# Cross-covariance attention with a gated FFN: softmax by blocks of the output columns, q's norm folded into the copy of the scores, G/H products in another order

## The chip, the cores and the metric

One core of one Trainium2 chip. The metric is the device time of one execution in microseconds. "Batch", "chunk" (512 tokens) and "step" (one of twelve blocks of 128 hidden units, f = 0 to 11) are the loops of the kernel.

## The reference, cut to what matters

```python
# q, k, v: (4, 6016, 256) float32; tau = 1
qn = q / (norm(q, axis=1) + 1e-6)            # norms over the 6016 tokens, one per column
kn = k / (norm(k, axis=1) + 1e-6)
s  = kn.transpose(0, 2, 1) @ qn / tau        # 256 x 256 per batch
a  = softmax(s)                              # over the last axis
x  = (v @ a).reshape(24064, 256)
out = (sigmoid(x @ w_gate) * (x @ w_val)) @ w_out     # w_gate, w_val: 256 x 1536
```

## The kernel before

`v @ a @ w_gate` is made as `v @ (a @ w_gate)`: per batch, the kernel makes G = a·w_gate and H = a·w_val (twelve products of 128x512, for three column groups `fg`, two matrices and two row blocks), then runs the gated FFN on the transposed v. The scores of batch b+1 are made inside the FFN of batch b; those of batch 0 have nothing to hide behind.

```python
    psg = pool("psg", 2, space=PSUM); psv = pool("psv", 2, space=PSUM)
    pso = pool("pso", 2, space=PSUM); pss = pool("pss", 1, space=PSUM)
    psm = pool("psm", 1, space=PSUM)            # one buffer
    ...
    def sums(b):                                # row sums of exp, both column blocks, one tile
        ps_r = psm.tile([P, CB], FP32, tag="m", name="ps_r")
        for i in range(CB):
            for j in range(CB):
                mm(ps_r[:, i : i + 1], s["e"][:, j, ds(i * P, P)], ones_bf[:, 0:1], ...)
        nc.vector.tensor_scalar(out=r, in0=ps_r, scalar1=1e-9, scalar2=None, op0=ALU.add)
        nc.vector.reciprocal(r, r)
    ...
    gh_order = [(fg, w, i) for fg in range(NFG) for w in range(2) for i in range(CB)]
    ...
    copy_s(0, 0); norms_inv(0); copy_s(0, 1)    # batch 0
    busy(12); spread_k(0); busy(10)             # busy: dummy matmuls
    scale_k(0)
    transpose_v(0, 0, ...)                      # by TensorE, copied out by VectorE
    exps(0)
    nc.scalar.preload_act_table(ACT.Sigmoid)
    sums(0)
    for n in range(4): gh(0, n, ...)            # four ahead, eight in steps 0 to 7
    ...
    at(11 * FC + 0, sums, n)                    # batches 1 to 3: in chunk 11 of the batch before
    for i in range(len(gh_order)): at(11 * FC + i, gh, n, i)
```

Cuts are marked with dots; several short lines are joined.

Of the kernel before, what the change touches and what calls it, by code (L numbers as in the profile page):

```python
# [9 lines left out]
FP32 = mybir.dt.float32  # L10
# [7 lines left out]
def kernel(  # L18
# [20 lines left out]
    nc = tc.nc  # L39
# [47 lines left out]
    def mm(out, lhsT, rhs, start, stop, **kw):  # L87
        nc.tensor.matmul(out, lhsT=lhsT, rhs=rhs, start=start, stop=stop, **kw)  # L88
# [75 lines left out]
            )  # L164
        return sq

    def norm_mms(ps, sqs, nt, first, last):

        for w, sq in enumerate(sqs):
            for u in range(nt):  # L170
                for j in range(CB):
                    mm(
                        ps[:, w * CB + j : w * CB + j + 1],
                        sq[:, u, ds(j * P, P)],
                        ones_bf[:, 0:1],
                        start=(first and w == 0 and u == 0 and j == 0),
                        stop=(last and u == nt - 1),
                        skip_group_check=True,
                    )
# [54 lines left out]
            )  # L234

    def copy_s(b, j):
        s = st[b]
        if j == 0:
            s["x"] = attp.tile([P, CB, C], FP32, tag="x", name="x_sb")
        nc.vector.tensor_copy(out=s["x"][:, j, :], in_=s["s"][:, j, :])  # L240

    def scale_k(b):
        s = st[b]
        for j in range(CB):
            x = s["x"][:, j, :]
            nc.vector.tensor_tensor(out=x, in0=x, in1=s["rk"], op=ALU.mult)  # L246

    def exps(b):
        s = st[b]
        s["e"] = attp.tile([P, CB, C], BF16, tag="e", name="e_sb", bufs=2)  # L250
        for j in range(CB):
            nc.scalar.activation(
                out=s["e"][:, j, :],
                in_=s["x"][:, j, :],
                func=ACT.Exp,
                bias=shift,
                scale=s["r"][:, j : j + 1],
            )

    def sums(b):  # L260
        s = st[b]
        ps_r = psm.tile([P, CB], FP32, tag="m", name="ps_r")
        for i in range(CB):
            for j in range(CB):
                mm(
                    ps_r[:, i : i + 1],
                    s["e"][:, j, ds(i * P, P)],
                    ones_bf[:, 0:1],
                    start=(i == 0 and j == 0),
                    stop=(j == CB - 1),  # L270
                    skip_group_check=True,
                )
        r = attp.tile([P, CB], FP32, tag="rrow", name="rrow", bufs=2)
        nc.vector.tensor_scalar(out=r, in0=ps_r, scalar1=1e-9, scalar2=None, op0=ALU.add)  # L274
        nc.vector.reciprocal(r, r)
        s["rrow"] = r
        s["gh"] = [
            [ghpool.tile([P, CB, FG], BF16, tag=f"{n}{fg}", name=f"gh_{n}{fg}") for fg in range(NFG)]
            for n in ("G", "H")
        ]  # L280

    gh_order = [(fg, w, i) for fg in range(NFG) for w in range(2) for i in range(CB)]

    def gh(b, n, pl=None, tag=None, act=0):
        s = st[b]
        fg, w, i = gh_order[n]
        ps = (pl or psm).tile([P, FG], FP32, tag=tag or "m", name="ps_gh")
        for j in range(CB):
            mm(
                ps,  # L290
                s["e"][:, j, ds(i * P, P)],
                w_sb[w][fg][:, j, :],
                start=(j == 0),
                stop=(j == CB - 1),
            )
        dst = s["gh"][w][fg][:, i, :]
        r = s["rrow"][:, i : i + 1]
        if n % 2 == act:
            nc.scalar.activation(out=dst, in_=ps, func=ACT.Copy, scale=r)  # L299
        else:  # L300
            nc.vector.tensor_scalar(out=dst, in0=ps, scalar1=r, scalar2=None, op0=ALU.mult)  # L301
# [1 line left out]

    vts = {}

    def transpose_v(b, ci, ps=None):

        t0, nt = groups[ci]
        v_sb = vs.pop((b, ci))
        vT = vtpool.tile([P, TPC * CB, P], BF16, tag="vT", name="vT")  # L310
        flat = v_sb[:, :nt, :].rearrange("p t c -> p (t c)")
        if ps is None:
            nc.sync.dma_start_transpose(out=vT[:, : nt * CB, :], in_=flat)
        else:
            for n in range(nt * CB):
                nc.tensor.transpose(
                    out=ps[:, n, :], in_=flat[:, ds(n * P, P)], identity=ident_bf
                )
            nc.vector.tensor_copy(out=vT[:, : nt * CB, :], in_=ps[:, : nt * CB, :])
        vts[b, ci] = vT.rearrange("p (u cb) n -> p cb u n", cb=CB)  # L320

    hts = {}
# [52 lines left out]
    def busy(n):  # L375

        ps = psg.tile([P, CH], FP32, tag="g", name="ps_busy")
        for _ in range(n):
            mm(ps[:, :P], ones_bf, ones_bf, True, True)
# [4 lines left out]
    for g in range(last0 + 2):  # L384
        if g <= last0:
            t0, nt = groups0[g]
            sq[g] = (
                squares(0, t0, nt, 0, nc.vector),
                squares(0, t0, nt, 1, nc.vector if g == last0 else nc.scalar),
            )  # L390
            for u in range(nt):
                score(0, t0, u)
        if g >= 1:
            norm_mms(ps_n0, sq.pop(g - 1), groups0[g - 1][1], g == 1, g == last0 + 1)
    st[0]["n"] = ps_n0
    norms_sqrt(0)
    nc.scalar.preload_act_table(ACT.Exp)
    copy_s(0, 0)
    norms_inv(0)
    copy_s(0, 1)  # L400
    busy(12)
    spread_k(0)
    busy(10)
    scale_k(0)
    transpose_v(0, 0, psv.tile([P, TPC * CB, P], BF16, tag="v", name="ps_tp"))
    exps(0)
    nc.scalar.preload_act_table(ACT.Sigmoid)
    sums(0)
    for n in range(4):
        gh(0, n, *((psg, "g"), (psv, "v"))[n % 2], act=1)  # L410


    def side_work(b):

        side = {}

        def at(slot, fn, *a):
            side.setdefault(divmod(slot, FC), []).append((fn, a))

        for ci in range(NCH):  # L420
            nb, nci = (b, ci + 1) if ci + 1 < NCH else (b + 1, 0)
            lb, lci = (b, ci + 2) if ci + 2 < NCH else (b + 1, ci + 2 - NCH)
            if (nb, nci) == (0, 1):
                at(7, lambda: transpose_v(0, 1, psm.tile([P, TPC * CB, P], BF16, tag="m", name="ps_tp")))
            elif nb < B:
                at(ci * FC + 2, transpose_v, nb, nci)
            if lb < B:
                at(ci * FC + 0, load_v, lb, lci)
        n = b + 1
        if n == B:  # L430
            return side
        first, last = (14 if b == 0 else 0), 9 * FC
        for g, (t0, nt) in enumerate(groups):
            s0 = first + g * (last - first) // NCH
            at(max(0, s0 - 20), load_qk, n, t0, nt)
            for u in range(nt):
                at(first + (t0 + u) * (last - first) // NT, score, n, t0, u)
            if g == 0:
                at(s0, acc_start, n)
            for i, (fn, w) in enumerate(((acc_square, 0), (acc_add, 0), (acc_square, 1), (acc_add, 1))):  # L440
                at(s0 + 1 + 2 * i, fn, n, g, w)
        at(9 * FC + 10, norms_mm, n)
        at(9 * FC + 11, norms_sqrt, n)
        at(10 * FC + 1, norms_inv, n)
        at(10 * FC + 2, spread_k, n)
        for j in range(CB):
            at(10 * FC + 1, copy_s, n, j)
        at(10 * FC + 4, scale_k, n)
        at(10 * FC + 11, exps, n)
        at(11 * FC + 0, sums, n)  # L450
        for i in range(len(gh_order)):
            at(11 * FC + i, gh, n, i)
        return side
# [3 lines left out]
    for b in range(B):  # L457
        side = side_work(b)
        for ci in range(NCH):
            block = b + 1 < B and ci in (9, 10)  # L460
            for f in range(FC):
                glu(b, ci, f)
                flush()
                if prev is not None and not block:
                    out_mms(*prev, f * TPC, (f + 1) * TPC)
                for fn, a in side.get((ci, f), ()):
                    fn(*a)
                if (b, ci) == (0, 0) and f < len(gh_order) - 4:
                    gh(0, 4 + f, pso, "o", act=1)
            if prev is not None and block:  # L470
                for s in range(TPC):
                    out_mms(*prev, s * FC, (s + 1) * FC)
                    flush()
            prev = (b, ci)
# [38 lines left out]
```

## Time and profile before

| | before |
|---|---|
| time, median of 6 runs | 841.4 us (839.7 to 842.1) |
| span of the profiled run | 837.4 us |
| square root of batch 0's norms starts | 35.22 us |
| second chunk's first gate product starts | 55.27 us |
| first sum to first G/H product, batch 1 | 0.64 us |

Lines of the timeline read: start in us, duration in us, engine, source line, operation, output <- inputs, and in brackets the idle time of that engine just before and what ended it. PE is TensorE, PEld its weight load, DVE VectorE, ACT ScalarE. PSUM is the memory that TensorE writes its products to. The tiles: e_sb holds the exp of the scores, ps_r its row sums, rrow their inverse; ps_gh is a G or H product in PSUM, gh_G and gh_H its copies; ps_gate and ps_val are the two products of a step, g_sb the sigmoid of the first, hT the product of both; vT is the transposed v.

### The profile page before, as it was taken

The numbers are of one execution on the slowest core, as the hardware profiler recorded it, in microseconds if no ns is written. First come the engines' busy times: TensorE is split into PE (matmuls) and PEld (weight loads), VectorE is DVE, ScalarE is ACT, GpSimd is POOL, SyncE is SP. The second block draws the span as 40 slices with busy tenths as digits, with TensorE's granted clock in tenths as the row PEclk, the third lists the DMA queues.
The fourth block names the chain that finished last, engine by engine and source line by source line (L and its number), as shares of the span: only waits on it lengthen the run. The fifth ranks groups of instructions, "written<-read, shape, count | busy, mean of one in ns | idle before, by whom it ended". The sixth has DMA issues, their size and how long they took to land.

```text
span 837.4 us, 13986 instructions
## 1 busy us (share of the span) xinstructions
PE 816.6 (98%) x5327; PEld 506.3 (60%) x5338; DVE 565.3 (68%) x976; ACT 389.3 (46%) x639; POOL 83.9 (10%) x161
## 2 busy tenths in 40 slices
PE   5899999999999999999999999999999999999998
PEld 4546666665666666665566666666566565656666
DVE  2477777776667777777656777777766666666664
ACT  3554444446544444444554444444654444444442
POOL 5532100002011100000210020000000000000000
PEclk9899999999999999999999999999999999999999
DMA  9999624227655543223864353223222522322211
GB/s 176 206 206 188 131 51 89 61 51 142 119 102 107 101 108 63 48 51 89 150 136 86 88 117 78 51 76 67 58 48 51 95 51 76 76 48 68 48 35 69
DMA packets 78738, 76.65 MB, mean 92 GB/s; under 512 B 50768, under 2 KB 55632, under 8 KB 78672
## 3 DMA queue, kind: packets, MB, share of 16 engines
q0 software_dynamic: 24208, 39.33, 28.4%
q1 hardware_dynamic: 54464, 36.45, 15.8%
q8 instruction: 41, 0.67, 0.3%
q14 instruction: 25, 0.20, 0.1%
HBM read 78.64 MB, written 24.64 MB: 123 GB/s over the span
## 4 chain that ended last, share of the span: by engine, by line
PE 91%; DMA 3%; DVE 2%; ACT 1%; issue 1%; POOL 0%; ACTq 0%; POOLq 0%
PE ps_o L88 29%; PE ps_gate L88 28%; PE ps_val L88 28%; PE ps_s L88 4%; DMA k_sb<-in_k_dram 3%; PE ps_gh L88 2%; DVE hT L344 1%; ACT g_sb L343 1%; PE ps_rk L88 0%; ACT gh_H L299 0%; DVE out_sb L370 0%; PE ps_n L88 0%; DVE gh_G L301 0%; DVE gh_H L301 0%; DVE x_sb L246 0%
## 5 line engine op out<-in xcount | busy, mean ns | idle before, releaser
L344 DVE TENSOR_TENSOR hT<-ps_val,g_sb 128x512 bf16<-128x512 f32 (+1 forms) x576 | 390.9, 679 | 220.1 <-ACT g_sb L343 216.2
L343 ACT ACTIVATE g_sb<-ps_gate 128x512 bf16<-128x512 f32 (+1 forms) x576 | 338.6, 588 | 400.0 <-PE ps_gate L88 387.6
L88 PE MATMUL ps_val<-vT,gh_H 128*128 128x512 bf16 (+1 forms) x1152 | 338.1, 375 | 0.5
L88 PE MATMUL ps_gate<-vT,gh_G 128*128 128x512 bf16 (+1 forms) x1152 | 337.5, 375 | 0.5
L88 PE MATMUL ps_o<-w_out_sb,hT 128*128 128x256 bf16 x2256 | 326.1, 273 | 0.0
L88 PEld LDWEIGHTS <-hT 128*128 128x128 bf16 x2256 | 220.7, 98 | 124.8
L88 PEld LDWEIGHTS <-gh_H 128*128 128x128 bf16 x1152 | 112.7, 98 | 132.9 <-ACT gh_H L299 1.5
L88 PEld LDWEIGHTS <-gh_G 128*128 128x128 bf16 x1152 | 112.4, 98 | 37.3 <-ACT gh_G L299 0.3
L370 DVE COPY out_sb<-ps_o 128x256 f32<-128x256 f32 x188 | 78.0, 415 | 20.9 <-PE ps_o L88 20.9
L106 POOL DMA_DIRECT2D v_sb<-in_v_dram x48 | 25.5, 531 | 631.3 <-DMA vT<-v_sb 496.3
L88 PE MATMUL ps_s<-k_sb,q_sb 128*128 128x256 bf16 x376 | 72.3, 295 | 12.2 <-DMA k_sb<-in_k_dram 12.2
L88 PEld LDWEIGHTS <-q_sb 128*128 128x128 bf16 x376 | 39.1, 104 | 20.3 <-issue 7.5
L162 DVE TENSOR_TENSOR sq<-q_sb 128x1024 bf16<-128x1024 bf16 (+3 forms) x46 | 30.4, 661 | 25.3 <-PE ps_n L88 19.1
L200 DVE TENSOR_TENSOR acc<-acc,sq 128x1024 bf16<-128x1024 bf16 (+1 forms) x66 | 44.1, 669 | 0.0
L97 POOL DMA_DIRECT2D k_sb<-in_k_dram x49 | 26.9, 549 | 14.5 <-DMA k_sb<-in_k_dram 9.1
L97 POOL DMA_DIRECT2D q_sb<-in_q_dram x49 | 26.8, 548 | 13.7 <-DMA q_sb<-in_q_dram 6.3
L162 DVE TENSOR_TENSOR sq<-k_sb 128x1024 bf16<-128x1024 bf16 (+2 forms) x34 | 22.4, 658 | 0.0
L160 ACT ACTIVATE sq<-k_sb 128x1024 bf16<-128x1024 bf16 (+1 forms) x12 | 12.2, 1021 | 20.1 <-DMA k_sb<-in_k_dram 19.7
L88 PE MATMUL ps_gh<-w_gate,e_sb 128*128 128x512 bf16 x41 | 12.8, 378 | 1.6 <-DVE rrow L274 1.2
L88 PEld LDWEIGHTS <-e_sb 128*128 128x128 bf16 x112 | 9.9, 97 | 6.8 <-issue 3.2
L88 PE MATMUL ps_gh<-w_val,e_sb 128*128 128x512 bf16 x44 | 13.2, 379 | 0.4
L299 ACT ACTIVATE gh_G<-ps_gh,rrow 128x512 bf16<-128x512 f32 x12 | 8.2, 687 | 9.7 <-PE ps_gh L88 5.6
(44 smaller groups left out, 99.7 us busy)
## 6 DMA issues: line engine op xcount, KB each, us to landing
out_dram<-out_sb SPq DMA_DIRECT2D x44, 512.0 KB, 2.9
q_sb<-in_q_dram POOLq DMA_DIRECT2D x44, 256.0 KB, 6.7
k_sb<-in_k_dram POOLq DMA_DIRECT2D x44, 256.0 KB, 7.6
v_sb<-in_v_dram POOLq DMA_DIRECT2D x44, 256.0 KB, 3.9
out_dram<-out_sb SPq DMA_DIRECT2D x4, 384.0 KB, 2.4
w_gate<-in_moe_w_gate_dram POOLq DMA_DIRECT2D x3, 256.0 KB, 7.0
w_val<-in_moe_w_val_dram POOLq DMA_DIRECT2D x3, 256.0 KB, 7.6
w_out_sb<-in_moe_w_out_dram POOLq DMA_DIRECT2D x1, 768.0 KB, 13.0
```

Source lines behind the costliest of these rows:

```text
L88: nc.tensor.matmul(out, lhsT=lhsT, rhs=rhs, start=start, stop=stop, **kw)
L97: nc.gpsimd.dma_start(out=tl[:, :nt, :], in_=rows(src, b)[:, t0 : t0 + nt, :])
L106: nc.gpsimd.dma_start(out=v_sb[:, :nt, :], in_=rows(v, b)[:, t0 : t0 + nt, :])
L160: nc.scalar.activation(out=sq[:, :nt, :], in_=src[:, :nt, :], func=ACT.Square)
L162: engine.tensor_tensor(out=sq[:, :nt, :], in0=src[:, :nt, :], in1=src[:, :nt, :], op=ALU.mult)
L200: nc.vector.tensor_tensor(out=acc[:, :nt, :], in0=acc[:, :nt, :], in1=st[b]["sq", w][:, :nt, :], op=ALU.add)
L299: nc.scalar.activation(out=dst, in_=ps, func=ACT.Copy, scale=r)
L343: nc.scalar.activation(out=g_sb[:, :n], in_=ps_gate[:, :n], func=ACT.Sigmoid)
L344: nc.vector.tensor_tensor(out=hts[b, ci][:, f, :n], in0=ps_val[:, :n], in1=g_sb[:, :n], op=ALU.mult)
L370: nc.vector.tensor_copy(out=out_sb[:, s, :], in_=ps)
```

## The change

It wants the start shorter. Exp, sums and G/H products go by blocks of 128 output columns, so that block 0 can go ahead while block 1 is still in exp; q's inverse norm is multiplied in while the scores are copied out of PSUM; six G/H products instead of four stand ahead of step 0; two copies and a square are shared between VectorE and ScalarE.

```diff
-        nc.vector.tensor_copy(out=s["x"][:, j, :], in_=s["s"][:, j, :])
+        nc.vector.tensor_scalar(out=s["x"][:, j, :], in0=s["s"][:, j, :],
+            scalar1=s["r"][:, j : j + 1], scalar2=None, op0=ALU.mult)
...
-    def sums(b):
-        ps_r = psm.tile([P, CB], FP32, tag="m", name="ps_r")
+    def sums(b, i, pl=psm, tag="m"):
+        ps_r = pl.tile([P, 1], FP32, tag=tag, name="ps_r")
...
-    gh_order = [(fg, w, i) for fg in range(NFG) for w in range(2) for i in range(CB)]
+    gh_order = [(fg, w, i) for fg in range(NFG) for i in range(CB) for w in range(2)]
...  # transpose_v
-            nc.vector.tensor_copy(out=vT[:, : nt * CB, :], in_=ps[:, : nt * CB, :])
+            half = nt * CB // 2
+            nc.vector.tensor_copy(out=vT[:, :half, :], in_=ps[:, :half, :])
+            (nc.scalar.copy if late is None else late)(vT[:, half : nt * CB, :], ps[:, half : nt * CB, :])
...  # start
+    exps(0, 0); exps(0, 1)
+    nc.scalar.copy(*late.pop())
+    sums(0, 0)
+    gh(0, 0, psg, "g", act=False); gh(0, 1, psv, "v", act=True)
     nc.scalar.preload_act_table(ACT.Sigmoid)
+    sums(0, 1, pss, "s")
+    gh(0, 2, psg, "g", act=False); gh(0, 3, psv, "v", act=False)
+    gh(0, 4, pso, "o", act=True);  gh(0, 5, pso, "o", act=False)
...  # batches 1 to 3
-        at(11 * FC + 0, sums, n)
+            at(11 * FC + 0, sums, n, i)      # for i in 0, 1
```

More of the change, by code (lines that the diff above doesn't have):

```diff
@@ L165, in squares, with norm_mms @@
         return sq
-    def norm_mms(ps, sqs, nt, first, last):
-        for w, sq in enumerate(sqs):
+    def norm_mms(ps, sqs, nt, first, last, order=(0, 1)):
+        for w in order:
+            sq = sqs[w]
             for u in range(nt):
@@ L175, in norm_mms @@
                         ones_bf[:, 0:1],
-                        start=(first and w == 0 and u == 0 and j == 0),
+                        start=(first and w == order[0] and u == 0 and j == 0),
                         stop=(last and u == nt - 1),
@@ L239, in copy_s @@
             s["x"] = attp.tile([P, CB, C], FP32, tag="x", name="x_sb")
-        nc.vector.tensor_copy(out=s["x"][:, j, :], in_=s["s"][:, j, :])
-    def scale_k(b):
-        s = st[b]
-        for j in range(CB):
-            x = s["x"][:, j, :]
-            nc.vector.tensor_tensor(out=x, in0=x, in1=s["rk"], op=ALU.mult)
-    def exps(b):
-        s = st[b]
-        s["e"] = attp.tile([P, CB, C], BF16, tag="e", name="e_sb", bufs=2)
-        for j in range(CB):
-            nc.scalar.activation(
-                out=s["e"][:, j, :],
-                in_=s["x"][:, j, :],
-                func=ACT.Exp,
-                bias=shift,
-                scale=s["r"][:, j : j + 1],
-            )
@@ L260, in sums @@
-    def sums(b):
-        s = st[b]
-        ps_r = psm.tile([P, CB], FP32, tag="m", name="ps_r")
-        for i in range(CB):
-            for j in range(CB):
-                mm(
-                    ps_r[:, i : i + 1],
-                    s["e"][:, j, ds(i * P, P)],
-                    ones_bf[:, 0:1],
-                    start=(i == 0 and j == 0),
-                    stop=(j == CB - 1),
-                    skip_group_check=True,
-                )
-        r = attp.tile([P, CB], FP32, tag="rrow", name="rrow", bufs=2)
+        nc.vector.tensor_scalar(
+            out=s["x"][:, j, :],
+            in0=s["s"][:, j, :],
+            scalar1=s["r"][:, j : j + 1],
+            scalar2=None,
+            op0=ALU.mult,
+        )
@@ new lines, in scale_k, with exps @@
+    def scale_k(b, i):
+        s = st[b]
+        x = s["x"][:, :, ds(i * P, P)]
+        rk = s["rk"][:, ds(i * P, P)].unsqueeze(1).to_broadcast([P, CB, P])
+        nc.vector.tensor_tensor(out=x, in0=x, in1=rk, op=ALU.mult)
+    def exps(b, i):
+        s = st[b]
+        e = attp.tile([P, CB, P], BF16, tag=f"e{i}", name=f"e_sb{i}", bufs=2)
+        nc.scalar.activation(
+            out=e, in_=s["x"][:, :, ds(i * P, P)], func=ACT.Exp, bias=shift
+        )
+        s.setdefault("e", []).append(e)
+        s.setdefault("rrow", [])
@@ L274, in sums @@
+    def sums(b, i, pl=psm, tag="m"):
+        s = st[b]
+        ps_r = pl.tile([P, 1], FP32, tag=tag, name="ps_r")
+        for j in range(CB):
+            mm(ps_r, s["e"][i][:, j, :], ones_bf[:, 0:1], j == 0, j == CB - 1)
+        r = attp.tile([P, 1], FP32, tag=f"rrow{i}", name="rrow", bufs=2)
         nc.vector.tensor_scalar(out=r, in0=ps_r, scalar1=1e-9, scalar2=None, op0=ALU.add)
         nc.vector.reciprocal(r, r)
-        s["rrow"] = r
-        s["gh"] = [
+        s["rrow"].append(r)
@@ L278, in sums, with gh_tiles @@
+    def gh_tiles(b):
+        st[b]["gh"] = [
             [ghpool.tile([P, CB, FG], BF16, tag=f"{n}{fg}", name=f"gh_{n}{fg}") for fg in range(NFG)]
@@ L280, in sums, with gh @@
         ]
-    gh_order = [(fg, w, i) for fg in range(NFG) for w in range(2) for i in range(CB)]
-    def gh(b, n, pl=None, tag=None, act=0):
+    gh_order = [(fg, w, i) for fg in range(NFG) for i in range(CB) for w in range(2)]
+    def gh(b, n, pl=None, tag=None, act=None):
         s = st[b]
@@ L290, in gh @@
                 ps,
-                s["e"][:, j, ds(i * P, P)],
+                s["e"][i][:, j, :],
                 w_sb[w][fg][:, j, :],
@@ L296, in gh @@
         dst = s["gh"][w][fg][:, i, :]
-        r = s["rrow"][:, i : i + 1]
-        if n % 2 == act:
+        r = s["rrow"][i]
+        if act if act is not None else n % 2 == 0:
             nc.scalar.activation(out=dst, in_=ps, func=ACT.Copy, scale=r)
@@ L304, with transpose_v @@
     vts = {}
-    def transpose_v(b, ci, ps=None):
+    def transpose_v(b, ci, ps=None, late=None):
         t0, nt = groups[ci]
@@ L386 @@
             t0, nt = groups0[g]
-            sq[g] = (
-                squares(0, t0, nt, 0, nc.vector),
-                squares(0, t0, nt, 1, nc.vector if g == last0 else nc.scalar),
-            )
+            engines = (nc.vector, nc.scalar) if g < last0 else (nc.scalar, nc.vector)
+            sq[g] = [squares(0, t0, nt, w, engines[w]) for w in range(2)]
             for u in range(nt):
@@ L393 @@
         if g >= 1:
-            norm_mms(ps_n0, sq.pop(g - 1), groups0[g - 1][1], g == 1, g == last0 + 1)
+            norm_mms(ps_n0, sq.pop(g - 1), groups0[g - 1][1], g == 1, g == last0 + 1, (0, 1) if g <= last0 else (1, 0))
     st[0]["n"] = ps_n0
@@ L397 @@
     nc.scalar.preload_act_table(ACT.Exp)
+    norms_inv(0)
     copy_s(0, 0)
-    norms_inv(0)
     copy_s(0, 1)
@@ L402 @@
     spread_k(0)
-    busy(10)
-    scale_k(0)
-    transpose_v(0, 0, psv.tile([P, TPC * CB, P], BF16, tag="v", name="ps_tp"))
-    exps(0)
-    nc.scalar.preload_act_table(ACT.Sigmoid)
-    sums(0)
-    for n in range(4):
-        gh(0, n, *((psg, "g"), (psv, "v"))[n % 2], act=1)
+    busy(4)
+    scale_k(0, 0)
+    scale_k(0, 1)
+    late = []
+    transpose_v(
+        0, 0, psv.tile([P, TPC * CB, P], BF16, tag="v", name="ps_tp"), lambda *a: late.append(a)
+    )
+    exps(0, 0)
+    exps(0, 1)
+    nc.scalar.copy(*late.pop())
+    gh_tiles(0)
+    sums(0, 0)
+    gh(0, 0, psg, "g", act=False)
+    gh(0, 1, psv, "v", act=True)
+    nc.scalar.preload_act_table(ACT.Sigmoid)
+    sums(0, 1, pss, "s")
+    gh(0, 2, psg, "g", act=False)
+    gh(0, 3, psv, "v", act=False)
+    gh(0, 4, pso, "o", act=True)
+    gh(0, 5, pso, "o", act=False)
     def side_work(b):
@@ L444, in side_work @@
         at(10 * FC + 1, norms_inv, n)
+        for j in range(CB):
+            at(10 * FC + 2, copy_s, n, j)
         at(10 * FC + 2, spread_k, n)
-        for j in range(CB):
-            at(10 * FC + 1, copy_s, n, j)
-        at(10 * FC + 4, scale_k, n)
-        at(10 * FC + 11, exps, n)
-        at(11 * FC + 0, sums, n)
+        for i in range(CB):
+            at(10 * FC + 4, scale_k, n, i)
+            at(10 * FC + 11, exps, n, i)
+            at(11 * FC + 0, sums, n, i)
+        at(11 * FC + 0, gh_tiles, n)
         for i in range(len(gh_order)):
@@ L467 @@
                     fn(*a)
-                if (b, ci) == (0, 0) and f < len(gh_order) - 4:
-                    gh(0, 4 + f, pso, "o", act=1)
+                if (b, ci) == (0, 0) and f < len(gh_order) - 6:
+                    gh(0, 6 + f, pso, "o")
             if prev is not None and block:
```

## The prediction

> **What bounds the kernel now.** I read the page first (busy times, chain), then the waits of TensorE, then the timeline of three stretches that the change touches: the start (0 to 56 us), the hand-over from one batch to the next (198 to 243 us), and the weight loads in the DMA view. From the page, the busy times and the chain by engine:
>
> ```profile
> PE 816.6 (98%) x5327; PEld 506.3 (60%) x5338; DVE 565.3 (68%) x976; ACT 389.3 (46%) x639; POOL 83.9 (10%) x161
> ...
> PE 91%; DMA 3%; DVE 2%; ACT 1%; issue 1%; POOL 0%; ACTq 0%; POOLq 0%
> ```
>
> TensorE is busy for 98% of the span and 91% of the chain. Only some 21 us of the span are open, and most lie in the start, while q and k of batch 0 arrive. Work taken from VectorE or ScalarE gains nothing unless TensorE waits for it. So the waits of TensorE by releaser come next:
>
> ```profile
> PE ps_s L88 <- DMA k_sb<-in_k_dram: 12.2, 11, 6.6
> PE ps_rk L88 <- DVE r L217: 1.2, 3, 0.4
> PE ps_gh L88 <- DVE rrow L274: 1.2, 3, 0.4
> PE ps_r L88 <- ACT e_sb L252: 0.3, 1, 0.3
> ```
>
> Columns: total, times, longest. 12.2 us are the loads of batch 0, which the change leaves alone. The softmax of batches 1 to 3 costs TensorE two waits of 0.4 us per batch: before the spread of k's norms, and after the row sums. The timeline shows the second (start, duration, instruction):
>
> ```profile
> 224.37 0.24 PE L88 MATMUL ps_r<-ones_bf,e_sb 128*128 128x1 bf16 x4
> 224.81 0.15 DVE L274 TENSOR_SCALAR rrow<-ps_r 128x2 f32<-128x2 f32 x1
> 224.99 0.17 DVE L275 RECIPROCAL rrow<-rrow 128x2 f32<-128x2 f32 x1
> 225.01 0.38 PE L88 MATMUL ps_gh<-w_gate,e_sb 128*128 128x512 bf16 x1 [0.40 <-DVE rrow L274]
> ```
>
> The sums and the G/H product share a PSUM pool of one buffer, so the product waits for VectorE to read the sums (224.81 to 224.96); it does not wait for the reciprocal. For batch 0, nothing hides the softmax:
>
> ```profile
> 37.13 1.09 ACT L252 ACTIVATE e_sb<-x_sb,shift,r 128x256 bf16<-128x256 f32 x2 [0.44 <-DVE x_sb L246]
> ...
> 38.24 1.28 ACT L407 ACT_TABLE_LOAD   x1
> ...
> 40.09 0.59 PE L88 MATMUL ps_gate<-vT,gh_G 128*128 128x512 bf16 x2
> ...
> 41.26 0.59 PE L88 MATMUL ps_gh<-w_gate,e_sb 128*128 128x512 bf16 x2
> ```
>
> Exps end at 38.22, the first gate product starts at 40.09, and at 41.26 TensorE has finished step f=0 and begins the fifth of twelve G/H products (eight are still to do). From there it runs densely except for two holes, both waits for ScalarE's copy of the last H block of a column group:
>
> ```profile
> 46.51 0.10 PEld L88 LDWEIGHTS <-gh_H 128*128 128x128 bf16 x1 [0.62 <-ACT gh_H L299]
> ...
> 52.45 0.10 PEld L88 LDWEIGHTS <-gh_H 128*128 128x128 bf16 x1 [0.62 <-ACT gh_H L299]
> ```
>
> In each, the pair of val products takes 0.90 us instead of 0.59: 0.31 us lost, 0.6 together. Check: from 41.26 to 55.27, where the second chunk starts, are 14.0 us. The work there is 8 G/H products of 0.432, 11 steps of 0.864 and eight transposes in 0.45, 13.4 us; the 0.6 is the rest.
>
> **What the Trainium skill says.** "ScalarE: Activation LUTs", section "What ACT_TABLE_LOAD costs", gives about 1283 ns for a load; the trace agrees, 1.28. It adds about 1380 ns of drain; the trace does not show that (load at 218.43, exp at 219.72). "PSUM — Partial Sum Buffer", section "PSUM bank collisions raise a hardware error", says no two engines may access one bank and quadrant at once, reads by ScalarE and VectorE included. No run yet shows it, but the built order of the changed kernel does it this way: ScalarE's half of the v-transpose copy waits for VectorE. "Perfetto Trace Analysis", section "Optimization Strategy", says to look for gaps on the contended engine in each regime and for the semaphore that ends them, which I do here.
>
> **The change part by part.**
>
> 1. *Start, softmax of batch 0.* The last q square goes to ScalarE beside VectorE's k square. Before, VectorE made both, ending at 34.92; now they overlap and end near 34.78: -0.15 us. Both score copies now come after the reciprocal, but the spread (to 36.63) covers them. Exp by column block lets the first sums start after the first exp (about 37.6, not 38.28). So G/H products can start 0.6 us sooner.
>
> 2. *Start, six G/H products ahead of step 0 instead of four.* Order now: fg0 G, H for block 0; G, H for block 1; then fg1 G, H for block 0. Products five and six need weights of the second column group. These are the issues of w_val in the timeline, and the DMA view of the stretch 33.1 to 33.3 (the last number is us from issue to landing):
>
> ```profile
> 33.18 0.71 POOL L130 DMA_DIRECT2D w_val<-in_moe_w_val_dram  x1
> ```
> ```profile
> w_val<-in_moe_w_val_dram POOLq DMA_DIRECT2D x1, 256.0 KB, 7.6
> ```
>
> It lands at 33.18 + 7.6 = 40.8; a k tile issued at 5.06 with 6.6 to landing was taken up by TensorE at 11.67, so landing and start agree. The sixth product cannot start before 40.8, and TensorE works in order, so step 0 starts at 40.8 + 0.43 = 41.2 and ends at 42.1. Before: 41.26. That is 0.84 us later with two products (0.86) fewer to do: **0**. What part 1 wins ends as a wait for this load. Sigmoid's table load moves behind the H copy (about 39.6 to 40.85), with the fifth product's copy after it to 41.5; gate 0 is not done before 41.8, so it is hidden.
>
> 3. *First chunk.* With two products more in hand, the H blocks are copied one step earlier than needed: the two holes go, **-0.6**.
>
> 4. *v transposes of chunk 1 (step 7).* Before, one VectorE copy:
>
> ```profile
> 50.63 0.61 PE L316 MATMUL ps_tp<-ident_bf,v_sb 128*128 128x128 bf16 x8
> ...
> 51.74 0.68 DVE L319 COPY vT<-ps_tp 128x1024 bf16<-128x1024 bf16 x1
> ```
>
> Now VectorE copies half (about 0.36 us, half of 0.68 and a little), behind its hT product of step 7 (ending near 51.8), and only then ScalarE the other half: about 52.1 to 52.7 (0.6, from a 128x512 sigmoid at 0.588). The sigmoid of step 8 comes after this in ScalarE's order: 52.7 instead of 51.8, 0.9 late. gate and val have two PSUM buffers each; gate 10 then waits for sigmoid 8 (53.3 against 52.9) and val 10 for its hT (54.0 against 53.8): **+0.7**.
>
> 5. *Hand-over of batches 1 to 3.* Two tiles of sums now go one after the other through the one-buffer pool, with nothing between on TensorE: sums 0, VectorE's add, sums 1, VectorE's add, product. The second round: sums 1 at 225.01, 0.22 to the result, add 0.15, two hand-overs of 0.03 to 0.04: +0.44 us, three times: **+1.3**. VectorE's copies of the scores and scalings have the same element counts (copies 0.36, scalings 0.37 each), exps the same 0.55; ScalarE still alternates with VectorE on the copies. The wait before the spread keeps its 0.4: the reciprocal stays where it was.
>
> Sum: 0 - 0.6 + 0.7 + 1.3 = +1.4 us. TensorE's matmul work is the same apart from six dummy matmuls fewer in the start, which do not set the end.
>
> **The rivals.**
> - *The start wins.* If ScalarE's copy does not delay sigmoid 8 enough to be felt, part 4 is 0; if the sixth load lands at 40.0, part 2 is -0.8. The change would be worth about -1.5 in the start and end near 842. For it: the edit is plainly aimed at the start. Against it: the landing above, and VectorE's hT ahead of the half copy.
> - *The sums' second round is hidden.* It would be if other matmuls lay between, or with a second buffer. The built order has none: the second sum waits for VectorE, and so does the product behind it. Without it the result is near 842.
> - *VectorE becomes the bound.* Scalings of 128x2x128 with a repeated operand from PSUM, if twice as slow, would add 0.74 us to VectorE per batch at step 4 of chunk 10, where TensorE already loses some 0.24 us to the scaling: up to +2.2 in all, 845.5. Against it: the same elements and the same form, only another stride.
> - *Slower TensorE clock* from the shorter dummy stretch (4 for 10): the transposes and sums follow at once, so no long idle comes of it; I give it little.
>
> **Range and chances.** 842.0 + 1.4 = 843.4; I take 843.3, a little lower since the start is the least certain part (each of its three terms may be off by 0.5) and such an edit was presumably meant to gain. Uncertainty of about 0.9 from the start, 0.3 from the hand-overs and 0.2 from run to run gives 841.9 to 844.5. A change of 2% is 16.8 us; nothing here reaches a fifth of that: 0.98 within 2%, 0.01 on each side.
>
> **What would show each step.** Part 2: TensorE waits for w_val near 40.8 with gate 0 near 41.2; wrong if gate 0 starts before 40.5. Part 3: no wait for gh_H in the first chunk. Part 4: ScalarE's copy of vT starts after VectorE's, and gates or vals of steps 9 to 11 show a gap of some 0.7 in all. Part 5: among TensorE's waits, ps_r for VectorE's add, three times 0.4, beside the old one; wrong if it is missing or hidden. The prediction falls if the second batch does not start later against its own first chunk, or if the first chunk ends over 0.7 us from 55.3.

## More of the kernel before

The time up to the square root is loading and scoring of batch 0; from there to the second chunk is its softmax, the G/H products and the first twelve steps. The profiled run of the kernel before took 839.55 us, a little less than any of the six.

## The result, and the profile after

| | before | after |
|---|---|---|
| time, median of 6 runs | 841.4 us (839.7 to 842.1) | 842.2 us (842.0 to 843.1) |
| square root of batch 0 | 35.22 us | 36.46 us |
| second chunk | 55.27 us | 56.51 us |
| from one to the other | 20.05 us | 20.05 us |
| first sum to first G/H product, batch 1 | 0.64 us | 1.08 us |

The ratio of the times is 1.0014 (95% interval 1.0001 to 1.0027), which is +1.2 us and within 2%. Ratios here are made from the fast runs of both kernels in the same rounds; they are not the ratio of the medians.

The page of the changed kernel, busy times and chain by engine, hardly differs:

```profile
PE 818.4 (97%) x5332; PEld 507.1 (60%) x5332; DVE 566.9 (67%) x984; ACT 389.4 (46%) x641; POOL 84.1 (10%) x161
...
PE 91%; DMA 3%; DVE 2%; ACT 2%; issue 1%; POOL 0%; ACTq 0%; POOLq 0%
```

TensorE's waits by releaser (total us, times, longest) tell more:

```profile
PE ps_r L88 <- DVE rrow L272: 1.3, 3, 0.4
PE ps_gh L88 <- DVE rrow L272: 0.8, 3, 0.3
PE ps_r L88 <- ACT e_sb L260: 0.6, 1, 0.6
PE ps_gate L88 <- ACT g_sb L345: 0.3, 1, 0.3
```

The first line is new: a second wait in each of the three hand-overs. The timeline of the first one, after:

```profile
225.61 0.19 PE L88 MATMUL ps_r<-ones_bf,e_sb 128*128 128x1 bf16 x2
...
226.05 0.15 DVE L272 TENSOR_SCALAR rrow<-ps_r 128x1 f32<-128x1 f32 x1
...
226.25 0.19 PE L88 MATMUL ps_r<-ones_bf,e_sb 128*128 128x1 bf16 x2 [0.45 <-DVE rrow L272]
...
226.47 0.16 DVE L272 TENSOR_SCALAR rrow<-ps_r 128x1 f32<-128x1 f32 x1
...
226.69 0.59 PE L88 MATMUL ps_gh<-w_gate,e_sb 128*128 128x512 bf16 x2 [0.25 <-DVE rrow L272]
```

Sum 0, add, sum 1, add, product: each needs the one PSUM buffer that the one before it holds. 1.08 - 0.64 = 0.44 us, three times 1.3.

The last line of the waits is the split copy of the v transposes at step 7:

```profile
52.91 0.41 DVE L320 COPY vT<-ps_tp 128x512 bf16<-128x512 bf16 x1
...
53.35 0.59 ACT L321 COPY vT<-ps_tp 128x512 bf16<-128x512 bf16 x1 [1.11 <-DVE vT L320]
...
53.84 1.09 ACT L345 ACTIVATE g_sb<-ps_gate 128x512 bf16<-128x512 f32 x2
...
54.49 0.59 PE L88 MATMUL ps_gate<-vT,gh_G 128*128 128x512 bf16 x2 [0.27 <-ACT g_sb L345]
...
55.22 0.59 PE L88 MATMUL ps_val<-vT,gh_H 128*128 128x512 bf16 x2
```

ScalarE idles 1.11 us until VectorE's half is done, then copies; the sigmoids come late; gate 10 starts at 54.49 instead of 54.05 (0.43 after val 9 at 53.62) and val 10 at 55.22 instead of 54.92: 0.74 us.

The two holes of the kernel before (val products of 0.90 us that waited for gh_H) are gone: every pair of val products of the first chunk takes 0.59 us. One weight load still idles for gh_H in step 0 (0.27 us at 42.67), without a hole in the matmuls.

In the two profiles the spans differ by 2.9 us, not 1.2. Where the rest lies is seen in the stretches view. Columns: stretch, its length, busy us (count) of PE, PEld, DVE, ACT and POOL, granted TensorE clock, DMA share, GB/s. Before:

```profile
33.00:34.00 1.00, 1.00 (x24) 0.94 (x22) 0.43 (x1) 0.62 (x2) 0.99 (x3) 1.00 1.20 222
34.00:35.00 1.00, 1.00 (x31) 0.91 (x29) 0.63 (x3) 0.35 (x1) 1.00 (x2) 1.00 1.15 194
```

After:

```profile
33.00:34.00 1.00, 1.00 (x10) 0.73 (x9) 0.00 (x0) 0.38 (x1) 0.99 (x3) 0.50 1.18 219
34.00:35.00 1.00, 1.00 (x21) 0.81 (x19) 0.42 (x1) 0.47 (x1) 1.00 (x2) 0.50 1.15 192
```

While the last scores of batch 0 were made, TensorE had its full clock in one run and half of it in the other. Up to the squares of the last group the instructions are the same in both kernels. The Trainium skill ("TensorE: Matmul & The Clock Gate", section "Part 1: The HAM clock gate (the "warmup" mystery)") says that a monitor halves or restores TensorE's clock by how busy it was in a free-running window of about 3.4 us, so that the moment varies from run to run. Both traces show such changes several times in the load phase: eight score matmuls take 1.86 us in some groups and 1.03 in others. In the changed kernel, for instance:

```profile
16.61 1.03 PE L88 MATMUL ps_s<-k_sb,q_sb 128*128 128x256 bf16 x8 [0.49 <-DMA k_sb<-in_k_dram]
...
19.18 1.86 PE L88 MATMUL ps_s<-k_sb,q_sb 128*128 128x256 bf16 x8 [1.16 <-DMA k_sb<-in_k_dram]
```

The scores of the last full group start at 32.22 before and at 32.26 after, so the loads are as early in both; from there the clock moved the square root by 1.24 us (35.22 to 36.46). Of the 2.9 us between the profiles, 1.24 are this accident, 1.3 the hand-overs, and the last 0.3 come after the last copy (833.67 before, 836.24 after: 2.57 apart), in the write of the output. So an accident as large as the effect can sit in any run of either kernel, and the experiments had to deal with it.

### The profile page after: what moved, and what is told of

Read it like the earlier page. It is cut to its first block, busy times and chain, and to the rows that moved or that the text cites. A ratio compares the mean times of both kernels' runs of the same rounds, so it can differ in the third digit from the quotient of the medians.

```text
span 840.3 us, 14002 instructions
## 1 busy us (share of the span) xinstructions
PE 818.4 (97%) x5332; PEld 507.1 (60%) x5332; DVE 566.9 (67%) x984; ACT 389.4 (46%) x641; POOL 84.1 (10%) x161
## 3 DMA queue, kind: packets, MB, share of 16 engines
q1 hardware_dynamic: 54464, 36.45, 16.5%
## 4 chain that ended last, share of the span: by engine, by line
PE 91%; DMA 3%; DVE 2%; ACT 2%; issue 1%; POOL 0%; ACTq 0%; POOLq 0%
PE ps_o L88 29%; PE ps_gate L88 28%; PE ps_val L88 28%; PE ps_s L88 4%; DMA k_sb<-in_k_dram 3%; PE ps_gh L88 2%; DVE hT L346 1%; ACT g_sb L345 1%; DVE gh_H L301 0%; PE ps_rk L88 0%; DVE out_sb L372 0%; PE ps_n L88 0%; ACT gh_G L299 0%; DVE x_sb L254 0%; ACT L417 0%
## 5 line engine op out<-in xcount | busy, mean ns | idle before, releaser
L162 DVE TENSOR_TENSOR sq<-q_sb 128x1024 bf16<-128x1024 bf16 (+2 forms) x45 | 30.1, 669 | 25.6 <-PE ps_n L88 19.5
L299 ACT ACTIVATE gh_G<-ps_gh,rrow 128x512 bf16<-128x512 f32 x22 | 15.1, 687 | 18.2 <-PE ps_gh L88 18.2
L301 DVE TENSOR_SCALAR gh_H<-ps_gh,rrow 128x512 bf16<-128x512 f32 x23 | 17.0, 742 | 0.0
```

Of the source, the lines that this page charges most:

```text
L162: engine.tensor_tensor(out=sq[:, :nt, :], in0=src[:, :nt, :], in1=src[:, :nt, :], op=ALU.mult)
L299: nc.scalar.activation(out=dst, in_=ps, func=ACT.Copy, scale=r)
L301: nc.vector.tensor_scalar(out=dst, in0=ps, scalar1=r, scalar2=None, op0=ALU.mult)
```

## The experiments

Theory: the change costs 1.3 us in the hand-overs of batches 1 to 3, and its start is worth nothing because a gain (two holes gone) meets an equal loss (the split copy). Rivals: the start alone is what differs; the extra VectorE instructions cost, not the buffer; or all of it is the clock's accident.

| run | median us | ratio to before (95%) | square root | second chunk | between | sum to product |
|---|---|---|---|---|---|---|
| e1 changed, sums in two pools | 841.36 | 1.0008 (0.9996 to 1.0021) | 36.74 | 57.15 | 20.41 | 0.64 |
| e2 before, sums split | 842.51 | 1.0025 (1.0011 to 1.0039) | 35.98 | 56.03 | 20.05 | 1.07 |
| e3 changed, one copy | 840.47 | 1.0003 (0.9991 to 1.0016) | 36.45 | 55.77 | 19.32 | 1.08 |
| e4 changed, warm | 841.13 | 1.0008 (0.9995 to 1.0020) | 35.28 | 55.21 | 19.93 | 1.08 |
| e5 before, warm | 839.72 | 0.9989 (0.9977 to 1.0002) | 35.58 | 55.63 | 20.05 | 0.64 |
| e6 changed, warm, two pools, one copy | 838.96 | 0.9980 (0.9967 to 0.9992) | 35.40 | 54.60 | 19.20 | 0.64 |
| e7 changed, warm, five ahead | 840.89 | 1.0003 (0.9989 to 1.0016) | 35.86 | 55.85 | 19.99 | 1.07 |
| e8 e6 and e7 together | 839.11 | 0.9980 (0.9968 to 0.9993) | 35.62 | 54.80 | 19.18 | 0.63 |
| e9 as e4 | 841.17 | 1.0009 (0.9995 to 1.0022) | 35.55 | 55.50 | 19.95 | 1.08 |
| e10 e9 with two pools | 839.92 | 0.9996 (0.9982 to 1.0010) | 36.75 | 56.61 | 19.86 | 0.64 |
| e11 e9 with one copy | 840.63 | 1.0005 (0.9992 to 1.0018) | 35.57 | 54.79 | 19.22 | 1.07 |
| e12 as e5 | 840.01 | 0.9995 (0.9981 to 1.0008) | 35.53 | 55.58 | 20.05 | 0.64 |

"Warm" means with the dummy matmuls of e4, which keep TensorE busy while batch 0 is loaded. The last four columns, in us, are from the profiled run of each. e1 to e4 and e9 to e12 ran on one chip, e5 to e8 on another. All results were correct.

### e1: the second sums in a pool of their own

```diff
-            at(11 * FC + 0, sums, n, i)
+            at(11 * FC + 0, sums, n, i, *((psm, "m"), (pss, "s"))[i])
```

> Changed kernel, but in batches 1 to 3 the sums of column block 1 get a PSUM buffer of their own. Theory (the hand-over through the one-buffer pool costs TensorE a second round trip of 0.44 us per batch): the wait of ps_r for VectorE's rrow add (three times 0.4 us) is gone, the start of the sums to the first G/H product falls from 1.08 us (225.61 to 226.69) to about 0.65, and the whole kernel is 1.3 us faster than the changed one, so about equal to the kernel before (ratio 0.9995 to 1.0005). Rival (the extra VectorE add and reciprocal are the cost, wherever the sums lie): the first product still starts about 1.0 us after the first sum and nothing is gained.

The wait is gone and the stretch from sum to product is 0.64 us, as the theory has it and against the rival. The time is another matter: 841.36 us, not the 840 of the kernel before. Its profile shows why that settles nothing: the half clock lasted at least to 37 us, the square root came at 36.74. The mechanism was shown, its worth in the time was not; e10 repeats it.

### e2: only the split of the sums, in the kernel before

```diff
+        if b == 0: ...as before...
+        else:
+            for i in range(CB):
+                ps_r = psm.tile([P, 1], FP32, tag="m", name="ps_r")
+                for j in range(CB):
+                    mm(ps_r, s["e"][:, j, ds(i * P, P)], ones_bf[:, 0:1], j == 0, j == CB - 1)
+                r = ...; add 1e-9; reciprocal
```

> The kernel before with that one part alone: in batches 1 to 3 each column block's sums get their own tile of the one-buffer pool; everything else is as before. Theory: ps_r waits for VectorE three times 0.4 us and the kernel is 1.3 us slower than before (ratio about 1.0016). Rival (the slowdown of the changed kernel comes from its start alone): ratio 1.0000, first product 0.64 us after the first sum as before.

The split alone brings the three waits of 0.45 us and makes the kernel slower (the interval excludes 1), against the rival. The ratio, 1.0025 or 2.1 us, is above the 1.3 expected, whose 1.0016 its interval does contain; the profiled run had its square root at 35.98, 0.76 later than the profile of before. Whether all of the excess is the clock, this run does not tell.

### e3: one copy of the transposes

```diff
-            half = nt * CB // 2
+            half = nt * CB // 2 if late is not None else nt * CB
             nc.vector.tensor_copy(out=vT[:, :half, :], in_=ps[:, :half, :])
-            (nc.scalar.copy if late is None else late)(...)
+            if late is not None: late(...)
```

> Changed kernel, but the transposes of chunk 1 are copied out by VectorE alone, as before. Theory (ScalarE's half comes after VectorE's and delays the sigmoid of step 8): the two holes of TensorE at steps 10 (gate 0.44, val 0.30 us) go, so from the first step's end to the second chunk is 0.7 us less than in the changed kernel (43.25 to 56.51, 13.26 us, becomes 12.5), and the kernel is 0.7 us faster than the changed one. Rival (VectorE is the limit there, since hT 7 and 8 and a whole copy of 0.68 come together): the same holes, now with VectorE as releaser, and no gain.

From square root to second chunk: 19.32 instead of 20.05 us, 0.73 less; no hole at step 10. VectorE did not take the place of ScalarE as the limit. The median of 840.47 cannot be set against the changed kernel's 842.2, which comes from other rounds; e11 repeats the experiment at a held clock.

### e4: a warm start

```diff
+            if 4 <= g <= 9:
+                busy(10 if g < 9 else 5)      # after the norm products of group g
```

> Changed kernel with 5 to 10 dummy matmuls after the norm products of groups 4 to 9 while q and k of batch 0 are loaded. Theory (the granted TensorE clock falls to 0.5 in the gaps of the load phase, by chance also for the last groups: 0.50 from 33 to 35 us in the changed kernel's profile, 1.00 in that of before; this moves the square root from 35.2 to 36.5): the last groups run at 1.00, the square root starts at 35.1 to 35.3 in the profile, the run is 1.2 us faster than the profile of the changed kernel and the spread between runs is smaller. With the start this early the sixth G/H product should wait for w_val of the second column group, landing near 40.8, and the first gate product start near 41.2. Rival (the late start is of the change itself, or the clock is not moved by such work): square root near 36.4 again, no gain.

The square root starts at 35.28, at full clock. Five timed runs lie between 840.75 and 841.22, where the kernel before has 839.5 to 841.2 in the same rounds; the profiled one, 840.75, is 1.27 us faster than that of the changed kernel, 842.02. Only with the start this early does the wait predicted for the weights appear:

```profile
40.67 0.59 PE L88 MATMUL ps_gh<-w_val,e_sb 128*128 128x512 bf16 x2 [0.26 <-DMA w_val<-in_moe_w_val_dram]
...
41.10 0.69 ACT L299 ACTIVATE gh_G<-ps_gh,rrow 128x512 bf16<-128x512 f32 x1
41.10 0.59 PE L88 MATMUL ps_gate<-vT,gh_G 128*128 128x512 bf16 x2
```

The first gate product follows at 41.10; 40.8 and 41.2 were predicted.

### e5 to e8: the pair at equal clock, both costs undone, five products ahead

e5 is the edit of e4 in the kernel before. e6 is e4 with the edits of e1 and e3. e7 is e4 with the sixth G/H product moved behind step 0; e8 is e6 and e7 together.

```diff
-    gh(0, 5, pso, "o", act=False)
...
-                if (b, ci) == (0, 0) and f < len(gh_order) - 6:
-                    gh(0, 6 + f, pso, "o")
+                if (b, ci) == (0, 0) and f < len(gh_order) - 5:
+                    gh(0, 5 + f, pso, "o")
```

> The kernel before with the same dummy matmuls in groups 4 to 9 as in e4: the pair with equal clock. Theory (at an equal clock the two kernels' starts are worth the same, and the change costs 1.3 us in the hand-overs): square root at 35.2, second chunk at 55.2 to 55.3, spread of runs under 0.6 us, and about 1.3 us faster than e4, so 839.8 where e4 had 841.1. Rival (the start of the changed kernel is itself a gain or a loss): e4 minus e5 differs from 1.3 by over 0.6, and the second chunk starts over 0.5 us from 55.2.

> e4 with both undone: sums of block 1 in a buffer of their own, transposes of chunk 1 copied by VectorE alone. Theory (two costs that add: 1.3 and 0.7 us): 2.0 us faster than e4, 0.7 faster than e5; second chunk at 54.5. Rival (one hides the other, or the clock made up the differences of e1 and e3): less than 1.2 us faster than e4.

> e4, but with five G/H products ahead of step 0 instead of six; the sixth goes behind step 0. Theory (at full clock the sixth product holds step 0 back until w_val of the second column group lands, and TensorE waited from 40.24 to 40.67 for it): first gate product at 40.2 to 40.4 instead of 41.10, no wait for w_val, second chunk 0.4 us earlier (54.8) and the kernel 0.4 us faster than e4. Rival (the eviction of G or the sigmoid behind the table load binds anyway): gate starts earlier, but the second chunk stays at 55.2.

> All together: warm start, a buffer for the second sums, one copy of the transposes, five products ahead. If the terms add: 0.4 + 0.7 + 1.3 = 2.4 us faster than e4, 1.1 faster than e5 and about 838.7; if five ahead wins nothing behind the others: 839.1. Second chunk at 54.1 or 54.5. It should then beat the kernel before and the changed one.

The kernel before, warm, needs 839.6 to 839.9 us. e6 is 0.76 us faster than it (medians), where 0.7 was expected. Against e4, e5 is 1.41 us faster (1.3 expected) and e6 2.17 (2.0 expected), but e4 ran on the other chip. The milestones of e5 came later than expected: square root at 35.58 instead of 35.2, second chunk at 55.63 instead of 55.3 at most. The clock was full there; the scores of the last full group start at 32.59, against 32.22 in the kernel before and 32.81 in e7, each just after a wait for their k tile. So the end of the loads moves the start too, by up to 0.6 us; the stretch from square root to second chunk leaves that out.

e7 missed: the wait for w_val went, the gate product started 4.96 us after the square root instead of 5.82, but nothing was gained by the second chunk (19.99 us against 19.93 and 19.95 of e4 and e9). Its timeline says where it went:

```profile
41.18 0.10 PEld L88 LDWEIGHTS <-gh_G 128*128 128x128 bf16 x1 [0.48 <-DVE gh_G L301]
...
41.84 0.10 PEld L88 LDWEIGHTS <-gh_H 128*128 128x128 bf16 x1 [0.55 <-DVE gh_H L301]
```

Step 0 now waits for VectorE's copies of G and H of block 1, which the wait for the weights had covered: its gate pair takes 0.75 us and its val pair 0.82 instead of 0.59 each, 0.39 together, which nearly eats up the 0.43 won (0.86 earlier, one product fewer done). The rival named for e7 was right. e8 accordingly equals e6 within its spread (839.11 and 838.96).

### e9 to e12: the parts at equal clock on one chip

> The kernel of e4 again, now on one chip with e10 to e12, since e4 and e5 ran on two chips and the clock's accidents in the start (over 1 us) hide what e1 and e3 were to show. It is the reference of this call: spread under 0.8 us; 1.2 us slower than e12 if the hand-overs cost 1.3 and the starts differ by -0.1.

> e9 with the second sums of batches 1 to 3 in a buffer of their own and nothing else. Theory (a second round trip of 0.44 us per batch, seen whole in the time): 1.3 us faster than e9 and equal to e12 within 0.3. Rival (part of the wait only moves): less than 0.9 us faster.

> e9 with the transposes of chunk 1 copied by VectorE alone and nothing else. Theory (ScalarE's half copy delays the sigmoid of step 8): no hole at steps 10 and 11, from the square root to the second chunk 19.2 us instead of 19.9, 0.7 us faster than e9. Rival: under 0.4 us.

> The kernel of e5 again, on the chip of e9 to e11: the change at equal clock. Theory: 1.2 us faster than e9. Rival (the measured slowdown of the change is an accident of the clock in the start): within 0.5 us of e9.

Against e9 (841.02 to 841.24), by medians: e10 is 1.25 us faster, e11 0.54, e12 1.16. e10 equals e12 within 0.1 us, so the second round trip shows whole in the time. One of e10's four runs, the profiled one, took 840.8 us; its stretches view and that of e9 show that the dummy matmuls make the full clock likely, not sure. Up to here the two programs are the same, and the scores of the last full group start at 32.50 and 32.52, yet the square root comes at 35.55 and 36.75: those 1.20 us are the clock alone. e9, then e10:

```profile
33.00:34.00 1.00, 1.00 (x23) 0.94 (x22) 0.25 (x1) 0.62 (x2) 0.99 (x2) 1.00 1.16 208
```
```profile
33.00:34.00 1.00, 1.00 (x7) 0.69 (x6) 0.00 (x0) 0.64 (x1) 0.98 (x2) 0.50 1.19 213
```

The hand-over of e10 (waits of TensorE are down to the one before the product, as in the kernel before):

```profile
225.72 0.24 PE L88 MATMUL ps_r<-ones_bf,e_sb 128*128 128x1 bf16 x4
...
226.16 0.15 DVE L272 TENSOR_SCALAR rrow<-ps_r 128x1 f32<-128x1 f32 x1
...
226.36 0.38 PE L88 MATMUL ps_gh<-w_gate,e_sb 128*128 128x512 bf16 x1 [0.40 <-DVE rrow L272]
...
226.42 0.14 DVE L272 TENSOR_SCALAR rrow<-ps_r 128x1 f32<-128x1 f32 x1
```

All four sum matmuls run together, and VectorE's second add is still there, but beside the product: the extra instruction costs nothing, the buffer did. In e11 step 10 follows step 9, whose val products start at 52.63, without a hole:

```profile
53.06 0.59 PE L88 MATMUL ps_gate<-vT,gh_G 128*128 128x512 bf16 x2
...
53.50 0.59 PE L88 MATMUL ps_val<-vT,gh_H 128*128 128x512 bf16 x2
```

The profile gains 19.95 - 19.22 = 0.73 us in the start; its runs spread from 840.4 to 841.8, so the 0.54 of the medians is less sure than the 0.73.

No experiment had the split copy without the order between the two engines, since both halves lie in one PSUM tile of 128x1024 bf16; that the order alone, and not ScalarE's copy as such, made the delay stays argued. The order is what the Trainium skill ("PSUM — Partial Sum Buffer", section "PSUM bank collisions raise a hardware error") asks of two engines on one bank and quadrant: ScalarE's half starts at 53.35, when VectorE's (52.91 for 0.41) has ended. Whether the error would be raised without it, no run shows.

## Why the prediction was right

**Hand-overs: right.** 0.44 us each was predicted and 0.44 measured; the time of e9 against e10 has 1.25 for the 1.3.

**Split copy: right.** +0.7 was predicted from the copies' order; 0.74 are in the trace, and e3 and e11 give 0.73 back.

**The two holes: right.** No pair of val products of the first chunk is stretched any more. The literal mark that the prediction set, no wait for gh_H, is met but for one short idle of a weight load in step 0.

**Six products ahead: the sum right, the reason half.** "0" was predicted, because step 0 would wait for w_val. At full clock it did so (0.26 us). In the profiled run it did not: the late start hid the load, and another wait stood there that I had called hidden, Sigmoid's table load. The timeline of the changed kernel:

```profile
41.22 1.28 ACT L417 ACT_TABLE_LOAD   x1
...
42.51 0.69 ACT L299 ACTIVATE gh_G<-ps_gh,rrow 128x512 bf16<-128x512 f32 x1
...
43.25 0.59 PE L88 MATMUL ps_gh<-w_gate,e_sb 128*128 128x512 bf16 x2
```

The copy of the fifth product waits for the table; the seventh product, which needs its buffer, starts at 43.25 instead of 42.95 (0.43 after val 0 at 42.52). In e9, at full clock, it was hidden as predicted: the copy starts at 41.37 and the seventh product follows val 0 without a hole. In e7 a third wait takes the place.

**Softmax of batch 0: two terms mis-sized, without effect on the end.** The square root was to come 0.15 us earlier; at equal clock it did not (35.55 in e9, 35.53 in e12), since VectorE's k square waits for norm products and starts at 34.91, where it had started at 34.94 behind the q square. And the first sums were to come at 37.6, "the spread covers" the copies: the pair of copies with the factor takes 0.88 us (from 36.25 in e9), not 0.72, and outlasts the spread, so the scaling starts 1.68 us after the square root instead of 1.45 in e12. Sums of a block start at 38.25 against 38.59 for the last sums in e12, 0.34 us earlier rather than 0.7. As predicted, this ended in the waits behind it. The exps, called the same 0.55 each, take 0.91 for two instead of 1.09: the Trainium skill ("ScalarE: Activation LUTs", section "What ACT_TABLE_LOAD costs") gives about 93 ns for each pointer operand, and the scale was one; the trace agrees with 0.09.

**The sum.** Start: +0.1 predicted, -0.1 measured at equal clock (19.95 - 20.05); hand-overs 1.3; together 1.2, as e9 and e12 differ by 1.16. The 0.2 by which the start came out better lie in part 2. The load of w_val lands a little earlier than estimated: the sixth product starts 5.39 us after the square root in e4 and e9 (40.67 and 40.94), where 40.8 - 35.22 = 5.58 was predicted. What the prediction had not seen is the accident of the clock, 1.2 us between two runs of one start; its range for run to run, 0.2, was too small for that. Its own last mark, that it falls if the first chunk ends over 0.7 us from 55.3, came true in the profiled run (56.51), and the wait for w_val was missing there. At full clock both are as predicted: 55.21 and 55.50 in e4 and e9, with 0.26 us of waiting for w_val in each.

That the measured +1.2 us came so near to the predicted +1.3 is in part luck: the interval of the ratio allows 0.1 to 2.3 us, and the 842.0 from which the prediction started was the median of three runs, where six give 841.4. The mechanism rests on the traces and on e9 to e12, not on that number.

## What to carry to other kernels

Splitting a small reduction into blocks for the sake of one exposed place also splits it where it was hidden; if its tiles share a one-buffer PSUM pool, each block can add a full round trip between two engines to TensorE's own order (0.44 us here). Before two engines share a copy out of PSUM, look whether the halves lie in one tile: here they went one after the other, and the sigmoid behind the second half paid. When an expected effect is around a microsecond, find milestones in the trace and make the start reproducible first; the version with dummy matmuls, two pools and one copy (e6) is the fastest measured here, 838.96 us, ratio 0.9980 to the kernel before.

## What the Trainium skill lacked or had wrong

- "TensorE: Matmul & The Clock Gate", section "HAM oscillation — how this bites in real kernels": as a rule it gives no idle gaps above about 3.4 us (its next section, "A second HAM failure mode: psum-queue depth-cycling", does name short idles as a cause, in another kind of kernel and without the length of a gap). In the changed kernel's load phase the clock fell to half with gaps of TensorE of at most 1.2 us (score matmuls of the group at 19.18 at half clock after a gap of 1.16 us, TensorE busy 3.35 of the 5 us before 20 us); with the dummy matmuls of e4 the clock stayed at 1.00 from 20 to 37 us, but in e10 the same ones did not prevent half clock in the scores at 32.52, after a gap of 0.88 us.
- The same page calls the ramp less than 1% of a span. Here it is 1.2 us of 840, which is true to that, and is yet as large as the whole effect of the change.
- "ScalarE: Activation LUTs", section "What ACT_TABLE_LOAD costs": the drain of about 1.38 us that it adds to a load does not show, neither before nor after it. The load at 41.22 follows an activation that ends at 41.20, takes 1.28 us, and the next activation starts at 42.51.
- "VectorE: DVE Perf Modes", section "The perf-mode tier table (the rule you actually need)", has tensor_copy and tensor_scalar in one row, and no page gives a time for a per-partition factor on VectorE. From PSUM in float32, a pair of 128x256 copies took 0.72 us before (chunk 10) and 0.87 to 0.88 with a per-partition factor: 0.08 us more each.
